# Backward of single-query attention: the V request moved between the two dV stores of a head, and the last V loaded in one piece

## The chip, the cores and the metric

One core of one Trainium2 chip, alone; the experiments ran on three chips (3, 7 and 10), each session beside the kernel before. The metric is the device time of one execution in microseconds (us). A core issues transfers through a queue (SP); the queue's transfers run on 16 DMA engines. A transfer of 128 partitions is 128 packets in the trace, eight for each engine, and sixteen semaphore increments, one from each engine.

## The reference, cut to what matters

```python
# q, grad_out: (1, 32, 1, 128); k, v: (1, 32, 8192, 128); all bf16
def fwd(q, k, v):
    scores = einsum('bhqd,bhkd->bhqk', q, k) * 128 ** -0.5
    attn = softmax(scores)
    return einsum('bhqk,bhkd->bhqd', attn, v)
out, vjp = jax.vjp(fwd, q, k, v)
return (out, *vjp(grad_out))        # out, dq, dk, dv
```

For each of 32 heads 2 MiB of K and 2 MiB of V are read and 2 MiB of dK and 2 MiB of dV are written: 268 MB in all.

## The kernel before

K and V tiles hold 64 rows in each of 128 partitions, so a partition's share of a load is one run of 16 KiB. Stores go in halves: 1 MiB, 8 KiB for each partition.

```python
K_BUFS, V_BUFS, NST = 3, 2, 2
def load_v(h):
    Vt[h] = vpool.tile([P, NT, D], BF16, tag="V", name="Vt")
    parts = NCH if h in (0, H - 1) else 1            # first and last V in four loads
    for c in range(parts):
        nc.sync.dma_start(slots(Vt[h], c, parts), rows_of(v, h, c, parts))

def outer(h, which, r):       # VectorE makes a quarter of dK or dV; after quarters 1 and 3 one half is stored
    ...
    if r % (4 // parts) == 4 // parts - 1:
        nc.sync.dma_start(rows_of(dst, h, c, parts), slots(G, c, parts))

for h in range(H + 1):        # ... marks cuts
    p_ = h - 1
    for u in range(NCH): k_blocks(h, u)              # VectorE transposes K
    k_scores(h)                                      # 64 small matmuls
    if 0 < h < H - 1: load_v(h + 1)
    ds_of(p_); outer(p_, "dk", 0); dq_of(p_, 0)      # 32 small matmuls
    s_mask(h); s_swap(h)
    dq_of(p_, 1); outer(p_, "dk", 1)                 # 32 small matmuls; first dK store
    if 0 < h and h + 2 < H: load_k(h + 2)
    ...                                              # softmax; dk 2, dk 3 and the second dK store
    v_transposes(h, 0)
    contract(Vt[h], x["p"], x["m"][:, 2:3])          # p times V: 64 small matmuls
    nc.scalar.copy(o_all[:, h:h + 1], x["m"][:, 2:3])
    v_transposes(h, 1)
    ...                                              # v_scores 0 to 3 (16 small matmuls each), transposes 2, 3
    outer(h, "dv", 0); outer(h, "dv", 1)             # first dV store
    outer(h, "dv", 2); outer(h, "dv", 3)             # second dV store
```

"Small" matmuls have 1, 2 or 4 columns and each comes with its own weight load of 128x128.

Of the kernel before, what the change touches and what calls it, by code (L numbers as in the profile page):

```python
# [24 lines left out]
def kernel(  # L25
# [13 lines left out]
    _, H, S, D = k.shape  # L39
    assert D == P and S % (P * CH) == 0 and H <= P  # L40
    NT = S // P
    NCH = NT // CH
# [20 lines left out]
    def rows_of(x, h, c, parts):  # L63
        L = NT // parts
        return x[0, h].rearrange("(p n) d -> p n d", p=P)[:, c * L:(c + 1) * L, :]

    def slots(X, c, parts):
        L = NT // parts
        return X[:, c * L:(c + 1) * L, :]

    def load_k(h):
        Kt[h] = kpool.tile([P, NT, D], BF16, tag="K", name="Kt")
        parts = NCH if h == 0 else 1
        for c in range(parts):
            nc.sync.dma_start(slots(Kt[h], c, parts), rows_of(k, h, c, parts))

    def load_v(h):
        Vt[h] = vpool.tile([P, NT, D], BF16, tag="V", name="Vt")
        parts = NCH if h in (0, H - 1) else 1
        for c in range(parts):  # L80
            nc.sync.dma_start(slots(Vt[h], c, parts), rows_of(v, h, c, parts))

# [54 lines left out]
    def k_blocks(h, u):  # L137


        if u == 0:  # L140
            XK[h] = ktpool.tile([P, CH, NB, NCH, QD], F32, tag="XK", name="XK_sb")
        nc.vector.transpose(XK[h][:, :, :, u, :],  # L142
                            slots(Kt[h], u, NCH).rearrange("p g d -> p (g d)").bitcast(F32).rearrange(
                                "p (g w j) -> p g w j", g=CH, w=NB))

    def k_scores(h):
        x = st[h]
        x["s"] = psS.tile([P, 512], F32, tag="s", name="s_ps")
        out = x["s"][:, 0:NT].rearrange("p (a g) -> p g a", a=NQ)
        cols = XK.pop(h).rearrange("p g w u i -> p (g w u i)").bitcast(BF16).rearrange(  # L150
            "p (g w ui e) -> p g w e ui", g=CH, w=NB, e=2)
        for g in range(CH):
            for c in range(2 * NB):
                nc.tensor.matmul(out[:, g, :], lhsT=cols[:, g, c // 2, c % 2], rhs=q_blk[:, h, c, :],  # L154
                                 start=(c == 0), stop=(c == 2 * NB - 1), skip_group_check=True)

    def s_mask(h):
        x = st[h]
        x["sm"] = small.tile([P, NQ, NCH, CH], F32, tag="sm", name="sm")
        nc.vector.tensor_tensor(  # L160
            x["sm"][:], x["s"][:, 0:NT].rearrange("p (a g) -> p a g", a=NQ).unsqueeze(2)
            .to_broadcast([P, NQ, NCH, CH]),
            in_quad[:].unsqueeze(1).unsqueeze(3).to_broadcast([P, NQ, NCH, CH]), op=ALU.mult)

    def s_swap(h):

        x = st[h]
        x["sn"] = x["s"][:, 128:128 + NT]
        for a in range(NQ):
            nc.tensor.matmul(x["s"][a * QD:(a + 1) * QD, 128:128 + NT], lhsT=lane[:],  # L170
                             rhs=x["sm"][:, a].rearrange("p u g -> p (u g)"),
                             start=True, stop=True, skip_group_check=True)
# [22 lines left out]
    def contract(Xt, rep, out_col, first=0, last=NT):  # L195
        for n in range(first, last):
            nc.tensor.matmul(out_col, lhsT=Xt[:, n, :], rhs=rep[:, n, 0:1],  # L197
                             start=(n == 0), stop=(n == NT - 1), skip_group_check=True)

    def outer(h, which, r):  # L200
        x = st[h]
        if r == 0:
            x[which] = gpool.tile([P, NT, D], BF16, tag=which, name="G_" + which)
        G, dst = x[which], out_2 if which == "dk" else out_3
        rep, row = x["ds"] if which == "dk" else x["p"], x["qd"][:, 0 if which == "dk" else 1, :]
        Q = NT // 4
        nc.vector.tensor_tensor(  # L207
            slots(G, r, 4).rearrange("p n (a b) -> p n a b", b=R),
            slots(rep, r, 4).unsqueeze(2).to_broadcast([P, Q, D // R, R]),
            row.rearrange("p (a b) -> p a b", b=R).unsqueeze(1).to_broadcast([P, Q, D // R, R]),  # L210
            op=ALU.mult)
        parts = 4 if h == H - 1 else NST
        if r % (4 // parts) == 4 // parts - 1:
            c = r // (4 // parts)
            nc.sync.dma_start(rows_of(dst, h, c, parts), slots(G, c, parts))
# [9 lines left out]
    def ds_of(h):  # L225
        x = st[h]
        pdt = small.tile([P, 1], F32, tag="pdt")
        nc.vector.tensor_copy(pdt[:], x["m"][:, 1:2])  # L228
        x["ds"] = small.tile([P, NT, R], BF16, tag="dsrep", name="ds_rep")
        nc.vector.scalar_tensor_tensor(  # L230
            out=x["ds"][:], in0=x["dp"][:, 0:NT].unsqueeze(2).to_broadcast([P, NT, R]), scalar=pdt[:],
            in1=x["p_s"][:].unsqueeze(2).to_broadcast([P, NT, R]), op0=ALU.subtract, op1=ALU.mult)

    def dq_of(h, half):
        out = st[h]["dp"][:, 128:129]
        contract(Kt[h], st[h]["ds"], out, half * NT // 2, (half + 1) * NT // 2)
        if half == 1:
            nc.scalar.copy(dq_all[:, h:h + 1], out)  # L238

    for h in range(H + 1):  # L240
        p_ = h - 1
        if h < H:
            x = st[h] = {}
            for u in range(NCH):
                k_blocks(h, u)
            k_scores(h)
            if 0 < h < H - 1:
                load_v(h + 1)
        if h > 0:
            ds_of(p_)  # L250
            outer(p_, "dk", 0)
            dq_of(p_, 0)
        if h < H:
            s_mask(h)
            s_swap(h)
        if h > 0:
            dq_of(p_, 1)
            outer(p_, "dk", 1)
        if 0 < h and h + 2 < H:
            load_k(h + 2)  # L260
        if h < H:
            mx = small.tile([P, 1], F32, tag="mx")
            nc.vector.reduce_max(mx[:], x["sn"], axis=AX.X)
            diag = small.tile([P, P], F32, tag="diag")
            nc.vector.tensor_scalar(diag[:], ident_f[:], mx[:], scale, op0=ALU.mult, op1=ALU.mult)
            x["m"] = psM.tile([P, 512], F32, tag="m", name="m_ps")
            nc.tensor.matmul(x["m"][:, 128:256], lhsT=ones_f[:], rhs=diag[:], start=True, stop=True,  # L267
                             skip_group_check=True)
            rows_bc(h)
        if h > 0:  # L270
            outer(p_, "dk", 2)
        if h == 0:
            load_k(2)
        if h < H:
            nbias = small.tile([P, 1], F32, tag="nbias")
            nc.vector.tensor_reduce(nbias[:], x["m"][:, 128:256], axis=AX.X, op=ALU.max, negate=True)  # L276
            e = small.tile([P, NT], F32, tag="e")
            rs = small.tile([P, 1], F32, tag="rs")
            nc.scalar.activation(e[:], x["sn"], ACT.Exp, bias=nbias[:], scale=scale, accum_out=rs[:])  # L279
            nc.tensor.matmul(x["m"][:, 0:1], lhsT=ones_f[:], rhs=rs[:], start=True, stop=True,  # L280
                             skip_group_check=True)
        if h > 0:
            outer(p_, "dk", 3)
        if h == H:
            break
        rinv = small.tile([P, 1], F32, tag="rinv")
        nc.vector.reciprocal(rinv[:], x["m"][:, 0:1])  # L287
        x["p"] = small.tile([P, NT, R], BF16, tag="prep", name="p_rep")
        nc.scalar.activation(x["p"][:], e[:].unsqueeze(2).to_broadcast([P, NT, R]), ACT.Copy, scale=rinv[:])  # L289
        x["p_s"] = small.tile([P, NT], F32, tag="p_s", name="p_s")  # L290
        nc.vector.tensor_scalar(x["p_s"][:], e[:], rinv[:], scale, op0=ALU.mult, op1=ALU.mult)
        v_transposes(h, 0)
        contract(Vt[h], x["p"], x["m"][:, 2:3])
        nc.scalar.copy(o_all[:, h:h + 1], x["m"][:, 2:3])
        v_transposes(h, 1)
        nc.tensor.matmul(x["m"][:, 1:2], lhsT=do_f[:, h:h + 1].to_broadcast([P, P]), rhs=o_all[:, h:h + 1],
                         start=True, stop=True, skip_group_check=True)
        v_scores(h, 0)
        v_transposes(h, 2)
        v_scores(h, 1)  # L300
        v_transposes(h, 3)
        v_scores(h, 2)
        v_scores(h, 3)
        outer(h, "dv", 0)
        outer(h, "dv", 1)
        outer(h, "dv", 2)
        outer(h, "dv", 3)

# [40 lines left out]
```

## Time and profile before

| | before |
|---|---|
| median of 4 runs | 663.08 us (662.32 to 663.71) |
| moved | 269.8 MB, 407 GB/s over the span |
| busiest compute engine | VectorE, 78% |
| a head in the steady part | 20.4 us |

The prediction below shows the DMA rows of the page, the stretches, the queue's waits and one head of the queue (start in us, duration in us, engine, line, operation, destination and sources, count), and says how to read them. One more view is needed for what follows. It is the trace's timeline of TensorE (start in us, duration in us, engine, line, operation, destination and sources, sizes, count), at the same head:

```profile
316.56 0.55 PE L192 MATMUL dp_ps<-do_blk,XT_sb 128*128 128x2 bf16 x16 [0.78 <-ACT XT_sb L182]
...
318.32 1.87 PE L154 MATMUL s_ps<-q_blk,XK_sb 128*128 128x4 bf16 x64 [1.21 <-DVE pdt L228]
320.05 0.99 PE L197 MATMUL dp_ps<-ds_rep,Kt 128*128 128x1 bf16 x32
320.97 0.44 PE L170 MATMUL s_ps<-sm,lane 128*32 128x64 f32 x8
321.34 1.01 PE L197 MATMUL dp_ps<-ds_rep,Kt 128*128 128x1 bf16 x32
```

From 318.3 to 322.3 us TensorE starts 136 matmuls and as many weight loads: some 68 instructions for each us. This is the densest stage of a head; I did not look at it when I predicted.

### The profile page before, as it was taken

The numbers are of one execution on the slowest core, as the hardware profiler recorded it, in microseconds if no ns is written. First come the engines' busy times: TensorE is split into PE (matmuls) and PEld (weight loads), VectorE is DVE, ScalarE is ACT, GpSimd is POOL, SyncE is SP. The second block draws the span as 40 slices with busy tenths as digits, with TensorE's granted clock in tenths as the row PEclk, the third lists the DMA queues.
The fourth block names the chain that finished last, engine by engine and source line by source line (L and its number), as shares of the span: only waits on it lengthen the run. The fifth ranks groups of instructions, "written<-read, shape, count | busy, mean of one in ns | idle before, by whom it ended". The sixth has DMA issues, their size and how long they took to land.

```text
span 662.2 us, 21100 instructions
## 1 busy us (share of the span) xinstructions
PE 505.4 (76%) x9705; PEld 470.8 (71%) x9705; DVE 513.4 (78%) x664; ACT 182.4 (28%) x321; POOL 0.7 (0%) x6
## 2 busy tenths in 40 slices
PE   2889888798887777878768687787877877768881
PEld 1878788688787766767668676677766777657871
DVE  5789788889987797777977778777788777786852
ACT  0332223223333222232222322223322323222330
POOL 0000000000000000000000000000000000000000
PEclk9955565757766576665567655666556665576655
DMA  8999999999999999999999999999999999999783
GB/s 335 410 424 427 426 421 422 423 423 427 427 425 426 426 424 427 427 428 424 426 422 428 426 426 429 420 428 415 413 423 418 414 416 415 396 424 402 290 355 144
DMA packets 29800, 269.83 MB, mean 407 GB/s; under 512 B 3472, under 2 KB 3472, under 8 KB 6032
## 3 DMA queue, kind: packets, MB, share of 16 engines
q1 hardware_dynamic: 29712, 268.48, 97.1%
q8 instruction: 76, 1.25, 0.7%
q14 instruction: 12, 0.10, 0.0%
HBM read 134.23 MB, written 134.23 MB: 405 GB/s over the span
## 4 chain that ended last, share of the span: by engine, by line
DMA 70%; PE 21%; DVE 3%; ACT 2%; issue 1%; SPq 0%; ACTq 0%
DMA Kt<-in_k_dram 26%; DMA Vt<-in_v_dram 25%; DMA out_dram<-G_dv 19%; PE T_ps L180 9%; PE s_ps L154 2%; PE m_ps L197 2%; PE dp_ps L197 2%; PE dp_ps L192 2%; ACT XT_sb L182 1%; DVE XK_sb L142 1%; PE m_ps L267 1%; PE m_ps L280 1%; DVE G_dk L207 1%; ACT e L279 1%; ACT qd L223 1%
## 5 line engine op out<-in xcount | busy, mean ns | idle before, releaser
L180 PE MATMUL T_ps<-ident_f,Vt 128*128 128x128 f32 x1024 | 222.6, 390 | 30.9 <-DMA Vt<-in_v_dram 30.8
L180 PEld LDWEIGHTS T_ps<-ident_f,Vt 128*128 128x128 f32 x1024 | 183.9, 208 | 32.1 <-issue 30.0
L142 DVE STREAM_TRANSPOSE XK_sb<-Kt 128x1024 f32<-128x1024 f32 x128 | 148.1, 1213 | 72.4 <-DMA Kt<-in_k_dram 72.3
L182 ACT COPY XT_sb<-T_ps 128x1024 f32<-128x1024 f32 x128 | 129.7, 1013 | 178.3 <-PE T_ps L180 178.3
L207 DVE TENSOR_TENSOR G_dk<-ds_rep,qd 128x2048 bf16<-128x2048 bf16 x128 | 155.7, 1219 | 1.1
L207 DVE TENSOR_TENSOR G_dv<-p_rep,qd 128x2048 bf16<-128x2048 bf16 x128 | 148.2, 1220 | 9.0 <-ACT p_rep L289 9.0
L192 PEld LDWEIGHTS <-XT_sb 128*128 128x128 bf16 x2048 | 73.3, 103 | 29.5 <-ACT XT_sb L182 27.5
L192 PE MATMUL dp_ps<-do_blk,XT_sb 128*128 128x2 bf16 x2048 | 71.6, 164 | 24.7 <-ACT XT_sb L182 24.7
L154 PE MATMUL s_ps<-q_blk,XK_sb 128*128 128x4 bf16 x2048 | 58.4, 167 | 28.8 <-DVE pdt L228 26.1
L154 PEld LDWEIGHTS <-XK_sb 128*128 128x128 bf16 x2048 | 55.8, 101 | 30.7 <-DVE pdt L228 27.9
L197 PE MATMUL dp_ps<-ds_rep,Kt 128*128 128x1 bf16 x2048 | 64.4, 165 | 7.1 <-issue 6.4
L197 PEld LDWEIGHTS <-Kt 128*128 128x128 bf16 x2048 | 59.7, 103 | 12.6 <-issue 12.4
L197 PEld LDWEIGHTS <-Vt 128*128 128x128 bf16 x2048 | 62.5, 105 | 2.0
L197 PE MATMUL m_ps<-p_rep,Vt 128*128 128x1 bf16 x2048 | 60.5, 166 | 0.0
L238 ACT COPY dq_all<-dp_ps 128x1 f32<-128x1 f32 x32 | 5.1, 159 | 178.2 <-PE dp_ps L197 178.2
L280 PEld LDWEIGHTS m_ps<-rs,ones_f 128*128 128x128 f32 x64 | 16.0, 311 | 48.6 <-ACT e L279 48.6
L280 PE MATMUL m_ps<-rs,ones_f 128*128 128x1 f32 x64 | 18.7, 362 | 39.2 <-ACT e L279 39.2
L276 DVE TENSOR_REDUCE nbias<-m_ps 128x1 f32<-128x128 f32 x32 | 9.3, 292 | 24.3 <-ACT qd L223 24.3
L267 PE MATMUL m_ps<-diag,ones_f 128*128 128x128 f32 x64 | 25.5, 499 | 2.2 <-issue 1.3
L230 DVE SCALAR_TENSOR_TENSOR ds_rep<-dp_ps,pdt,p_s 128x256 bf16<-128x256 f32 x32 | 15.5, 484 | 14.0 <-PE dp_ps L192 11.8
L289 ACT ACTIVATE p_rep<-e,rinv 128x256 bf16<-128x256 f32 x32 | 16.2, 508 | 30.3 <-DVE rinv L287 30.3
L223 ACT CAST qd<-m_ps 128x256 bf16<-128x256 f32 x32 | 11.9, 373 | 44.8 <-PE m_ps L219 44.8
(44 smaller groups left out, 161.0 us busy)
## 6 DMA issues: line engine op xcount, KB each, us to landing
Kt<-in_k_dram SPq DMA_DIRECT2D x31, 2048.0 KB, 27.7
out_dram<-G_dv SPq DMA_DIRECT2D x62, 1024.0 KB, 25.6
out_dram<-G_dk SPq DMA_DIRECT2D x62, 1024.0 KB, 27.8
Vt<-in_v_dram SPq DMA_DIRECT2D x30, 2048.0 KB, 28.1
Vt<-in_v_dram SPq DMA_DIRECT2D x8, 512.0 KB, 13.7
Kt<-in_k_dram SPq DMA_DIRECT2D x4, 512.0 KB, 5.1
out_dram<-G_dv SPq DMA_DIRECT2D x4, 512.0 KB, 16.8
out_dram<-G_dk SPq DMA_DIRECT2D x4, 512.0 KB, 10.3
```

Source lines behind the costliest of these rows:

```text
L142: nc.vector.transpose(XK[h][:, :, :, u, :], slots(Kt[h], u, NCH).rearrange("p g d -> p (g d)").bitcast(F32).rearrange("p (g w j) -> p g w ...
L154: nc.tensor.matmul(out[:, g, :], lhsT=cols[:, g, c // 2, c % 2], rhs=q_blk[:, h, c, :], start=(c == 0), stop=(c == 2 * NB - 1), skip_group ...
L180: nc.tensor.transpose(T_ps[:, i, :], words[:, m * P:(m + 1) * P], ident_f[:])
L182: nc.scalar.copy(X[:], T_ps[:])
L192: nc.tensor.matmul(st[h]["dp"][:, n:n + 2], lhsT=X[:, i, e2, :], rhs=do_blk[:, h, e2, :], start=(e2 == 0), stop=(e2 == 1), skip_group_chec ...
L197: nc.tensor.matmul(out_col, lhsT=Xt[:, n, :], rhs=rep[:, n, 0:1], start=(n == 0), stop=(n == NT - 1), skip_group_check=True)
L207: nc.vector.tensor_tensor(slots(G, r, 4).rearrange("p n (a b) -> p n a b", b=R), slots(rep, r, 4).unsqueeze(2).to_broadcast([P, Q, D // R, ...
L223: nc.scalar.copy(x["qd"][:].rearrange("p a d -> p (a d)"), x["m"][:, 256:512])
L230: nc.vector.scalar_tensor_tensor(out=x["ds"][:], in0=x["dp"][:, 0:NT].unsqueeze(2).to_broadcast([P, NT, R]), scalar=pdt[:], in1=x["p_s"][: ...
L267: nc.tensor.matmul(x["m"][:, 128:256], lhsT=ones_f[:], rhs=diag[:], start=True, stop=True, skip_group_check=True)
L280: nc.tensor.matmul(x["m"][:, 0:1], lhsT=ones_f[:], rhs=rs[:], start=True, stop=True, skip_group_check=True)
L289: nc.scalar.activation(x["p"][:], e[:].unsqueeze(2).to_broadcast([P, NT, R]), ACT.Copy, scale=rinv[:])
```

## The change

Its intent: V(h+2) is asked for as soon as V(h)'s buffer can be free, ahead of the second dV store, and the queue alternates loads and stores better. The last V no longer needs to come in pieces.

```diff
     def load_v(h):
-        parts = NCH if h in (0, H - 1) else 1
+        parts = NCH if h == 0 else 1
@@
             k_scores(h)
-            if 0 < h < H - 1:
-                load_v(h + 1)
@@
         outer(h, "dv", 0)
         outer(h, "dv", 1)
+        if h + 2 < H:
+            load_v(h + 2)
         outer(h, "dv", 2)
         outer(h, "dv", 3)
```

## The prediction

> **What bounds the kernel now.** I read the page's DMA rows first: 268 MB pass through one core, and no compute engine is above 78% busy.
>
> ```profile
> span 662.2 us, 21100 instructions
> DMA  8999999999999999999999999999999999999783
> GB/s 335 410 424 427 426 421 422 423 423 427 427 425 426 426 424 427 427 428 424 426 422 428 426 426 429 420 428 415 413 423 418 414 416 415 396 424 402 290 355 144
> q1 hardware_dynamic: 29712, 268.48, 97.1%
> q8 instruction: 76, 1.25, 0.7%
> ```
>
> The plateau is some 425 GB/s with every DMA engine over 90% busy; the last slices fall off. At 425 GB/s 268.5 MB take 632 us, so 30 us seem to be lost, and the fall at the end looks like where. The second view, stretches of the trace with the DMA share and GB/s last, shows what that fall is:
>
> ```profile
> 165.00:440.00 275.00, 212.14 (x4104) 197.98 (x4103) 216.83 (x272) 79.06 (x139) 0.00 (x0) 0.61 1.01 426
> 440.00:590.00 150.00, 113.83 (x2265) 106.06 (x2261) 117.22 (x150) 39.77 (x71) 0.00 (x0) 0.59 1.01 415
> 655.00:660.00 5.00, 0.00 (x0) 0.00 (x0) 0.00 (x0) 0.00 (x0) 0.00 (x0) 0.50 0.06 26
> ```
>
> At 655 to 660 us one engine of 16 (share 0.06 = 1/16) still moves 26 GB/s, its full rate, and the other fifteen are done. So I grouped the trace's semaphore increments from DMAs in sixteens, one for each DMA engine of a transfer. The last increment of each transfer trails the fifteenth by 0.15 us at 14.7 us, 3.0 us at 204 us, 7.5 us at 389 us, 11.1 us at 594 us and 6.7 us at the end; the earliest is 20 us ahead by 460 us. One DMA engine is late for the whole run, and no transfer counts as landed before it. The landings of that engine follow each other without a hole from 14.7 us to 660.9 us: about 2.5 us for a 1 MiB store, 4.9 us for a 2 MiB load, up to 6.3 us where instruction fetches fall in.
>
> Its work can be added up. Each engine carries 1/16: 64 loads x 8 packets of 16 KiB and 128 stores (counted as 1 MiB) x 8 packets of 8 KiB. The trace's packets last 611 and 309 ns at the median and overlap by 4 ns: 512 x 0.607 + 1024 x 0.305 = 623 us, and some 2 us for 209 semaphore packets. The 76 fetch packets never overlap one another; beside one of them a store packet typically lasts 0.70 us and a load packet 1.10 us, so about 0.45 us is lost at each, 34 us in all if one engine takes them (not shown by a record, but the sum fits): 623 + 2 + 34 = 659, after a start at 1.7 us gives 660.9. The last bulk landing is at 660.9. This engine has no idle time to win.
>
> The third view is the DMA queue's own waits, 165 to 590 us (total us, times, longest):
>
> ```profile
> SPq L215 <- DMA Kt<-in_k_dram: 93.6, 21, 5.1
> SPq L215 <- DMA out_dram<-G_dk: 91.1, 42, 2.3
> SPq L75 <- DMA Vt<-in_v_dram: 86.8, 20, 4.5
> SPq L215 <- DMA out_dram<-G_dv: 52.9, 21, 2.6
> SPq L81 <- DMA out_dram<-G_dv: 46.2, 21, 2.9
> SPq L215 <- DVE mx L263: 3.2, 5, 2.0
> ```
>
> Nearly all of it is one transfer waiting for another, not for compute. The program has eight DMA semaphores in turn, so transfer n waits for transfer n-8 to land. One head of the steady state as the queue issues it:
>
> ```profile
> 313.68 2.99 SPq L215 DMA_DIRECT2D out_dram<-G_dv  x2
> 318.88 0.34 SPq L81 DMA_DIRECT2D Vt<-in_v_dram  x1
> 321.81 0.33 SPq L215 DMA_DIRECT2D out_dram<-G_dk  x1
> 326.67 0.34 SPq L75 DMA_DIRECT2D Kt<-in_k_dram  x1
> 329.20 0.33 SPq L215 DMA_DIRECT2D out_dram<-G_dk  x1
> ```
>
> A head lasts 20.42 us (313.68 to the next at about 334.1, and the same spacing for most heads), while a clean one costs a DMA engine 16 x 0.607 + 32 x 0.305 = 19.5 us; the 0.9 us between them is 76/32 = 2.4 fetches. At each issue seven older transfers are still pending, 23 to 25 us of work for the late engine.
>
> **What the Trainium skill says.** "DMA: Bandwidth & Descriptors", section "Why a DMA increments its semaphore by 16 and not by 1": every participating engine posts its own increment and only the full 16 means landed. The trace agrees, and the spread of those sixteen is the 11 us above. Same page, "Issuing engines are not separate DMA queues": all issued DMAs end on the same 16 engines; so order in the queue cannot make bandwidth. "Perfetto Trace Analysis", section "Roofline", puts one core alone at the 16 engines' aggregate of about 435 GB/s; the plateau here is 426. "Runtime: NRT & Kernel Launch", section "Instruction fetch mechanics": each sequencer refills its instructions in 16 KiB blocks of 256 through a DMA queue of its own. The trace agrees with the block (76 packets, 1.25 MB); the page calls the cost mostly hidden, which is true for the sequencer but not, by the sum above, for the late DMA engine.
>
> **The change, part by part.** I compared the built instruction streams. PE, DVE and ACT keep every instruction in its place; only the semaphores that they wait on are renumbered. So fetch traffic is the same, 0 us.
>
> 1. "Two heads ahead" is a new name for almost the same place. Before, V of head h+1 was issued in head h after K's scores, and the queue ran dV(h-1), dV(h-1), V(h+1), dK(h-1). Now it runs dV, V, dV, dK: one 2 MiB load passes one 1 MiB store. Bytes and packets are the same. In steady state V lands about 2.5 us earlier and the second dV half 4.9 us later. The late engine sees the same sum in another order: 0 us.
>
> 2. The wait for V's buffer. V(h+2) takes the buffer of V(h), free after PE's last transposes of head h. Early in the run this holds the queue: the first dV store is issued at 22.72 us, V at 28.58. The second dV half, which went at about 25, must now wait for 28.9. Does an engine run dry? At 28.6 us the fastest engine has just finished the third K (landings 28.8 to 31.4) and has dV's first half, 2.5 us, to go; V is then in the queue. In the next head V is issued at 47.7 while about 3 us (fastest) to 6 us (late engine) remain. Later the backlog grows. No hole: 0 us, at worst under 1 us once, on engines that have slack later.
>
> 3. G_dv's buffers. DVE may write G_dv(h) only when both stores of head h-2 have landed. The second one landed about 4.3 us before it was needed in steady state (321.7 against 326.06); now it lands about 4.9 us later, so DVE may wait about 0.5 us for it. DVE sat idle for 3.4 us before K's transposes and dV's issue comes 8 us later, so this is hidden.
>
> 4. The last V in one load instead of four. Three fewer transfers: three semaphore packets of some 10 ns each. It also frees the queue at the end, which before spent 10.65 us on it:
>
> ```profile
> 594.07 0.34 SPq L75 DMA_DIRECT2D Kt<-in_k_dram  x1
> ...
> 606.70 10.65 SPq L81 DMA_DIRECT2D Vt<-in_v_dram  x4
> 621.93 2.93 SPq L215 DMA_DIRECT2D out_dram<-G_dk  x2
> ...
> 646.92 4.44 SPq L215 DMA_DIRECT2D out_dram<-G_dk  x4
> ```
>
> The dK stores at 621.93 waited for the last K to land; eight places on there is now another transfer, so they should go at about 610. That feeds the fifteen fast engines earlier, not the late one, which has its backlog anyway. The final chain is K landed (621.89), transposes, scores, V's transposes at 633.39, dK, last store at about 651. Is the unsplit V there in time? On the late engine after K at 621.87 follow dK's half (2.6), dV's half (2.6), V (4.9): about 632.0, 1.4 us before PE wants it. And were it late, the last store goes out at 651 while the late engine has work until 660.9: some 9 us of slack.
>
> Sum: 0 + 0 + 0 + 0, with a few tenths either way. I take 663.3 us against 663.4.
>
> **The rivals.**
> (a) The end is bound by compute and the unsplit V delays it. For: the page's chain ends in K's landing, PE and DVE work, and the split was there for that. Against: 9 us of slack on the late engine. It would take a V over 10 us late; say 665 to 668.
> (b) The holes in the last slices are starvation by the queue, and freeing it wins. For: 290 and 144 GB/s, and 12 us of earlier dK stores. Against: one engine at 26 GB/s to the very end. If the fetches moved with the order of transfers or the late engine did have holes, up to 10 us could come: 653.
> (c) V's buffer wait in front of the second dV half starves the DMA in the first 165 us, where the queue waits for compute. For: the wait exists (up to 4 us at a time). Against: the backlog of 3 us and more. A loss of 1 us in each of 8 heads would give 671.
>
> **Range and chances.** Three runs before lie between 662.32 and 663.71; with half a microsecond for steps 2 and 3 and for another session I take 661.7 to 665.0. Over 2% would mean beyond 650 or 677, further than any rival is likely to reach: faster 0.01, same 0.97, slower 0.02.
>
> **What would show it.** Right: 20.4 us for a steady head; one engine at 26 GB/s at the end; the median landing time of dK stores down by up to 2.5 us and of dV stores up by as much; dK stores near 610 us instead of 621.93; the DMA row full from the second slice. Wrong: a slice below 400 GB/s before 150 us (c), PE waiting for the last V after 634 us and the last store after 660 (a), or the late engine done before 655 (b).

## The result, and the profile after

| | before | changed |
|---|---|---|
| median | 663.08 us | 657.43 us (656.14 to 658.36) |
| ratio | | 0.9914, 95% interval 0.9893 to 0.9935 |

Ratios are computed as the mean time of one kernel's runs over that of the other's of the same rounds, so they are not quite the ratio of the medians. By the 2% rule the two are the same, as forecast; but the gain of 5.7 us is clear of the noise and lies outside my range of 661.7 to 665.0.

First the changed kernel's page, the rows that answer to those of before:

```profile
span 656.6 us, 21096 instructions
GB/s 334 408 389 428 424 422 430 420 423 430 424 424 428 425 428 423 428 424 427 428 424 426 428 424 425 428 428 423 428 425 424 431 421 426 419 418 412 374 339 149
q8 instruction: 76, 1.25, 0.7%
```

The third slice fell from 424 to 389 GB/s (a hole at the start), bytes and fetches are the same, and the plateau now stays near 424 until the 36th slice, where before it had sagged to 415 from the 28th on. Then the same stretches (DMA share and GB/s last):

```profile
165.00:440.00 275.00, 222.40 (x4135) 208.07 (x4136) 219.93 (x276) 79.00 (x140) 0.00 (x0) 0.56 1.01 426
440.00:590.00 150.00, 121.25 (x2266) 112.98 (x2264) 118.67 (x151) 41.30 (x76) 0.00 (x0) 0.53 1.01 424
651.00:654.00 3.00, 0.00 (x0) 0.00 (x0) 0.00 (x0) 0.00 (x0) 0.00 (x0) 0.50 0.06 26
```

Still one DMA engine of sixteen works alone at the end, at its full 26 GB/s. So the bound is the one that I had named. It simply finished 5.7 us earlier. The queue's timeline of one head says where (the lines of before have 20.4 us from head to head):

```profile
313.14 0.33 SPq L215 DMA_DIRECT2D out_dram<-G_dv  x1
315.75 0.34 SPq L81 DMA_DIRECT2D Vt<-in_v_dram  x1
318.27 0.33 SPq L215 DMA_DIRECT2D out_dram<-G_dv  x1
323.12 0.33 SPq L215 DMA_DIRECT2D out_dram<-G_dk  x1
325.65 0.34 SPq L75 DMA_DIRECT2D Kt<-in_k_dram  x1
328.42 0.33 SPq L215 DMA_DIRECT2D out_dram<-G_dk  x1
333.27 0.33 SPq L215 DMA_DIRECT2D out_dram<-G_dv  x1
```

A head now takes 333.27 - 313.14 = 20.13 us. The landings of K add it up: from K of head 9 to K of head 31 the kernel before needs 621.9 - 170.8 = 451.1 us and the changed one 616.9 - 172.0 = 444.9, 6.2 us less over 22 heads. K of head 9 itself is 1.2 us later, and the rest after head 31 is 0.7 us shorter.

To see which transfer got cheaper I took, for each transfer, the last of its sixteen semaphore increments, and the step from one transfer's last increment to the next: the time that the late engine spent on it. Near 310 to 330 us:

```
before:  V 4.86   dK 2.53   K 4.91   dK 2.65   dV 2.54   dV 2.91     sum 20.40
changed: dK 2.60  dV 2.52   V 4.85   dV 2.53   dK 2.75   K  4.86     sum 20.11
clean:   a load 8 x 0.607 = 4.86, a store 8 x 0.305 = 2.44           sum 19.48
```

Loads cost their clean time to within 0.05 us. Nearly everything above it, 0.9 us before and 0.6 us now, is lost in stores, and in the kernel before half of it in one store, the second dV half. That half was being moved from about 318.3 to 321.2 us (an increment comes some 0.5 us after its last packet), which is TensorE's densest stage shown above. In the changed kernel TensorE's timeline reads:

```profile
317.78 1.87 PE L154 MATMUL s_ps<-q_blk,XK_sb 128*128 128x4 bf16 x64 [1.52 <-DVE pdt L228]
319.51 0.99 PE L197 MATMUL dp_ps<-ds_rep,Kt 128*128 128x1 bf16 x32
320.43 0.44 PE L170 MATMUL s_ps<-sm,lane 128*32 128x64 f32 x8
320.80 1.01 PE L197 MATMUL dp_ps<-ds_rep,Kt 128*128 128x1 bf16 x32
...
326.28 1.89 PE L197 MATMUL m_ps<-p_rep,Vt 128*128 128x1 bf16 x64
```

The dense stage, 317.8 to 321.8 us, now lies under the V load (the late engine moved it from 317.7 to 322.6), and the second dense stage, p times V at 326.3 to 328.2, under the first dK store (325.1 to 327.8), whose step is now the dearest, 2.75 us.

Packets of one DMA engine follow each other without a gap, so the eight packets of a transfer on the late engine can be followed back from its last increment (some that could not be followed are left out). Sorted by the number of TensorE matmuls and weight loads that start while a packet lasts, their mean duration in ns (number of packets):

```
instructions started     0-7         8-21        22-29       30 or more
store 8 KiB, before      318 (469)   339 (147)   357 (177)   388 (47)
store 8 KiB, changed     317 (601)   337 (83)    350 (129)   389 (11)
load 16 KiB, before      613 (217)   620 (37)    611 (32)    620 (106)
load 16 KiB, changed     614 (131)   619 (47)    620 (60)    614 (162)
```

On this engine a store packet gets up to 22% longer in TensorE's dense stages (388 against 318 ns), a load packet 1% at most. The changed order moved dense stages from stores to loads: store packets with 22 or more went from 224 to 140. An instruction fetch somewhere on the 16 engines does not slow it: before, its store packets beside a fetch lasted 333 ns (70 of them), without one 334 ns; and none of its steps from 130 to 550 us is longer by as much as a fetch packet (0.9 us): the longest store step there is 3.28 us.

### The profile page after: what moved, and what is told of

It reads as the page before. It is cut to its first block, busy times and chain, and to the rows that moved or that the text cites. A ratio compares the mean times of both kernels' runs of the same rounds, so it can differ in the third digit from the quotient of the medians. Undisturbed runs are those within 1.5% of the kernel's fastest.

```text
span 656.6 us, 21096 instructions
## 1 busy us (share of the span) xinstructions
PE 520.1 (79%) x9705; PEld 485.8 (74%) x9705; DVE 513.8 (78%) x664; ACT 182.2 (28%) x321; POOL 0.7 (0%) x6
## 4 chain that ended last, share of the span: by engine, by line
DMA 63%; PE 23%; DVE 8%; ACT 2%; issue 1%; SPq 0%; ACTq 0%; DVEq 0%
DMA Kt<-in_k_dram 35%; DMA out_dram<-G_dv 29%; PE T_ps L180 10%; DVE XK_sb L142 6%; PE s_ps L154 3%; PE dp_ps L197 2%; PE m_ps L197 2%; PE dp_ps L192 2%; ACT XT_sb L182 1%; PE m_ps L265 1%; PE m_ps L278 1%; DVE G_dk L207 1%; ACT e L277 1%; ACT qd L223 1%; PE s_ps L170 1%
## 5 line engine op out<-in xcount | busy, mean ns | idle before, releaser
L180 PE MATMUL T_ps<-ident_f,Vt 128*128 128x128 f32 x1024 | 237.8, 410 | 0.0
L180 PEld LDWEIGHTS T_ps<-ident_f,Vt 128*128 128x128 f32 x1024 | 198.8, 222 | 0.0
L207 DVE TENSOR_TENSOR G_dv<-p_rep,qd 128x2048 bf16<-128x2048 bf16 x128 | 148.2, 1220 | 14.0 <-DMA out_dram<-G_dv 10.7
L192 PEld LDWEIGHTS <-XT_sb 128*128 128x128 bf16 x2048 | 77.5, 107 | 30.2 <-ACT XT_sb L182 27.1
L192 PE MATMUL dp_ps<-do_blk,XT_sb 128*128 128x2 bf16 x2048 | 73.8, 166 | 24.3 <-ACT XT_sb L182 24.3
L265 PE MATMUL m_ps<-diag,ones_f 128*128 128x128 f32 x64 | 25.6, 500 | 2.3 <-issue 1.7
## 6 DMA issues: line engine op xcount, KB each, us to landing
out_dram<-G_dv SPq DMA_DIRECT2D x62, 1024.0 KB, 25.3
out_dram<-G_dk SPq DMA_DIRECT2D x62, 1024.0 KB, 25.3
```

The lines of the kernel that those rows point to most:

```text
L180: nc.tensor.transpose(T_ps[:, i, :], words[:, m * P:(m + 1) * P], ident_f[:])
L192: nc.tensor.matmul(st[h]["dp"][:, n:n + 2], lhsT=X[:, i, e2, :], rhs=do_blk[:, h, e2, :], start=(e2 == 0), stop=(e2 == 1), skip_group_chec ...
L207: nc.vector.tensor_tensor(slots(G, r, 4).rearrange("p n (a b) -> p n a b", b=R), slots(rep, r, 4).unsqueeze(2).to_broadcast([P, Q, D // R, ...
L265: nc.tensor.matmul(x["m"][:, 128:256], lhsT=ones_f[:], rhs=diag[:], start=True, stop=True, skip_group_check=True)
```

## The experiments

The theory: one DMA engine, always the same, sets the end; its stores, and not its loads, slow down while TensorE starts many instructions. (The increments carry no engine number. That the last one is always the same engine's is read from its lag, which grows smoothly from about 125 us on in both kernels.) Rivals: the unsplit last V made the gain; the instruction fetches of the prediction slow the late engine; the exchange of order matters in itself; a busy TensorE slows it, whatever its instructions. Twelve kernels ran.

**The change in two halves.** First the new order with the last V still in four loads.

```diff
-        parts = NCH if h == 0 else 1
+        parts = NCH if h in (0, H - 1) else 1
```

> The new order alone, the last V still in four loads. Theory: on the DMA engine that lands last, a store packet takes 309 ns while TensorE starts few instructions and up to 389 ns in its dense stages, a load packet 611 ns always; the new order puts a V load under the densest stage, so the steady head falls from 20.4 to 20.1 us and the whole gain comes from here: 657 to 658 us. Rival: the gain comes from the unsplit last V, which frees the queue at the end: then 663 us here.

Measured: 657.15 us, ratio to before 0.9909 (0.9894 to 0.9923). Then the other half, in the kernel before:

```diff
-        parts = NCH if h in (0, H - 1) else 1
+        parts = NCH if h == 0 else 1
```

> The old order, the last V in one load. Theory: 663 us, the steady head stays at 20.4 us. Rival (the unsplit last V makes the gain): 657 to 658 us.

Measured: 663.24 us, ratio 1.0002 (0.9988 to 1.0017). The whole gain comes from the order; the last V is worth nothing.

**TensorE moved, the queue left alone.** In the changed kernel one group of transposes goes ahead of p times V:

```diff
         v_transposes(h, 0)
+        v_transposes(h, 1)
         contract(Vt[h], x["p"], x["m"][:, 2:3])
         nc.scalar.copy(o_all[:, h:h + 1], x["m"][:, 2:3])
-        v_transposes(h, 1)
```

> The changed kernel with one exchange on TensorE alone: the second group of V transposes goes before the 64 small matmuls of p times V. The DMA queue keeps its order, and instructions, bytes and fetches are the same. Theory: those matmuls move by 1.8 us, from under the first dK store (step 2.75 us on the late engine) to under the K load, so that step falls to about 2.5 us, the head from 20.13 to 19.9 us, the whole by 4 to 6 us against the changed kernel: 652 to 654 us. Rivals (instruction fetches slow the late engine; or only the order of transfers counts): no change, 657 to 658 us.

Measured: 653.75 us, ratio 0.9867 (0.9846 to 0.9888), 3.7 us under the changed kernel (ratios 0.9867 against 0.9914). Its TensorE timeline at another head:

```profile
303.19 3.59 PE L180 MATMUL T_ps<-ident_f,Vt 128*128 128x128 f32 x16
306.61 1.76 PE L197 MATMUL m_ps<-p_rep,Vt 128*128 128x1 bf16 x64
```

The 64 small matmuls start at 306.6; the K load is moved from about 306.4 to 311.3 us (the first dK half has its last increment at 306.86, K at 311.78). The first dK store's mean step between 250 and 590 us fell from 2.79 to 2.53 us and the other stores stayed within 0.03. Not one instruction, byte or fetch was added or taken away.

The same exchange in the kernel before is the control:

> Control: the same exchange on TensorE (second group of V transposes before the 64 matmuls of p times V) in the kernel before. There these matmuls already lie under the K load, about 1.5 us after its start, and stay under it when they move by 1.8 us. Theory: no change, 663 us within 1.5. Rival (the exchange is good for TensorE or ScalarE in itself, whatever the DMA moves): 659 to 660 us, as with the changed kernel.

Measured: 662.66 us, ratio 0.9989 (0.9973 to 1.0006): no change, as expected, since there p times V lay under the K load already. So the exchange is not good in itself.

**Which engine is late.** In the changed kernel one store was cut into 16:

```diff
+            if h == 24 and which == "dv" and c == 0:
+                p0 = 0
+                for n in (15, 14, 13, 12, 11, 10, 9, 8, 7, 6, 5, 4, 3, 2, 1, 8):
+                    nc.sync.dma_start(rows_of(dst, h, c, parts)[p0:p0 + n], slots(G, c, parts)[p0:p0 + n])
+                    p0 += n
```

> One 1 MiB store of head 24 cut by partitions into 16 stores of 15, 14, 13 ... 1 and 8 partitions, to learn by their landings on which of the 16 DMA engines the late one is: a store of n partitions takes n engines[...]. Those with the late engine should land about 8 us after the others' level, those without it early. Time within 2 us of the changed kernel, 656 to 659 us. If no single engine is late (rival: the lateness moves from engine to engine), the landings show no such edge.

Measured: 661.51 us (one run), slower than expected, because the small stores used up the eight places of the queue and the backlog ran out. The stores of 15 down to 9 partitions all had one late increment, so the late engine is one of the numbers 0 to 8; below that nothing could be read. The second probe keeps the backlog:

```diff
+            if 17 <= h <= 24 and which == "dv" and c == 0:
+                for n in (h - 16, 32 - h, 112):     # n, 16-n and 112 partitions
+                    nc.sync.dma_start(...[p0:p0 + n], ...[p0:p0 + n])
```

> A second probe for the number of the late DMA engine (the first leaves 0 to 8, because its small stores let the backlog run out), on the changed kernel with the exchange: in heads 17 to 24 the first dV store is cut into n, 16-n and 112 partitions, n = 1 to 8, so that the backlog stays. The smallest store that has an increment 4 us or more after all others tells the number. Time 654 to 658 us.

Measured: 663.28 us (one run), again slower than I expected. The landings answer the question. The stores of 1, 2, 3 and 4 partitions were complete 12.4, 10.5, 8.5 and 7.7 us before the whole dK store that was issued ahead of them, so the late engine had no part in them; that of 5 partitions had its last increment 6.9 us after the one before it, and landed level with the late engine (458.90 us, between dK at 458.60 and the next piece at 459.23). With the rule that the Trainium skill gives ("DMA: Bandwidth & Descriptors", section "Why a DMA increments its semaphore by 16 and not by 1": the lowest-numbered k engines), the late engine is number 4. The trace agrees with the rule as far as it shows it: one increment for each partition of these small stores, and one more at once.

**More of the disputed work, under loads or under stores.** Twins with p times V run twice for each head, in one under the K load, in the other under stores:

```python
# the order after the edit; ... marks cuts
# under the load                          # under the stores
v_transposes(h, 0)                        contract(... [:, 2:3])
v_transposes(h, 1)                        contract(... [:, 3:4])   # not used
contract(... [:, 2:3])                    nc.scalar.copy(o_all ...)
contract(... [:, 3:4])   # not used       v_transposes(h, 0)
nc.scalar.copy(o_all ...)                 v_transposes(h, 1)
```

> Changed kernel; the 64 small matmuls of p times V are run twice (the second result is not used), both after the second group of V transposes, so from 3.6 to 7.1 us after the softmax, under the K load. 2048 more matmuls with their weight loads, some 16 more instruction fetches. Theory: a load packet does not mind TensorE, so about the time of the exchange alone plus a little for the longer chain of compute: 653 to 657 us. Rival (fetches, or the number of TensorE instructions in itself, slow the late engine): the same as its twin with both under the stores.

Measured: 695.92 us, ratio 1.0502 (1.0456 to 1.0549).

> Twin of the other: the same instructions, both runs of the 64 matmuls before the first V transposes, from the softmax's end to 3.5 us later, under the second dV store and the first dK store. Theory: the late engine loses about 0.25 us more for each steady head than in the changed kernel (its dK step 2.8 us and its dV step 2.7 us or more), 661 to 666 us, 5 to 10 us over the twin. Rival: no difference between the twins.

Measured: 667.53 us, ratio 1.0063 (1.0048 to 1.0078). The opposite of the forecast, and no test of the theory, because the bound changed. The chain that ended last in the twin under the load, shares by engine:

```profile
PE 81%; ACT 9%; DVE 5%; issue 3%; DMA 1%; SPq 0%; DVEq 0%; ACTq 0%
```

In both the queue waited for compute (in the first for V's transposes 249.9 us in 30 waits, in the second 225.4 us in 30), and near 310 us the late engine was only 0.2 to 0.7 us behind the fifteenth in the first, 2.7 to 3.4 us in the second. I had counted on 1.5 us of idle TensorE for 1.7 us of added work. The pair says only that there is no room for more compute.

**Less of it.** With 1 of the 64 matmuls left (wrong results), first in the kernel before:

```diff
-        contract(Vt[h], x["p"], x["m"][:, 2:3])
+        nc.tensor.matmul(x["m"][:, 2:3], lhsT=Vt[h][:, 0, :], rhs=x["p"][:, 0, 0:1], start=True, stop=True, ...)
```

> Wrong result on purpose: in the kernel before, only 1 of the 64 matmuls of p times V is left for each head (2016 matmuls and as many weight loads fewer, some 15 instruction fetches fewer). In its steady state these matmuls lie under the K load. Theory: the late engine gains little, 661 to 663.5 us. Rival (fetches, or the number of TensorE instructions, slow the late engine): 15 fetches of 0.45 us, 656 to 657 us.

Measured: 658.04 us, ratio 0.9925 (0.9911 to 0.994). More than I expected, and near the rival's number.

> The same cut in the changed kernel, where these matmuls lie under the first dK store. Theory: that store's step on the late engine falls from 2.8 to about 2.5 us, the whole by 4 to 6 us against the changed kernel, 651 to 654 us, a larger gain than in the kernel before. Rival: the same gain in both kernels.

Measured: 646.39 us, ratio 0.9746 (0.973 to 0.9763): 11 us under the changed kernel, 5.9 us more than the same cut saved in the kernel before. The rival asks for the same gain in both and falls by that. The mean steps of the late engine show what happened (us, transfers landing between 250 and 590):

```
                     dK 1st  dK 2nd  dV 1st  dV 2nd   V     K
before               2.57    2.68    2.59    2.92     4.86  4.92
before, one matmul   2.53    2.60    2.50    2.93     4.86  4.90
changed              2.79    2.61    2.57    2.50     4.87  4.88
changed, exchange    2.53    2.61    2.60    2.51     4.87  4.90
changed, one matmul  2.45    2.47    2.54    2.53     4.95  4.93
```

In both, the shorter TensorE chain also pulled the bursts of V scores forward, out of the second dK and first dV half (0.08 and 0.09 us in the kernel before, whose whole head fell from 20.54 to 20.32 us, 4.8 us over 22 heads). That term I had left out. The second dV half under the densest stage stayed at 2.93 us although 16 fetches and 4032 TensorE instructions were gone. In the last row the late engine is hardly late any more: near 320 us it is 0.2 us behind the fifteenth, against 3.3 us in the changed kernel, and its store packets last 310 ns at the mean.

**The cost by itself.** A kernel without the attention: the queue always full of 1 MiB stores from one tile, with compute in stages.

```diff
+    for _ in range(16): store()
+    g = gate(1)                       # a small load that starts the next stage when it lands
+    for _ in range(16): store()
+    for _ in range(1200): nc.tensor.matmul(ps[:, 0:1], lhsT=g[:], rhs=wide[:, 0:1], ...)
+    ...                               # 90 matmuls of 512 columns; 300 VectorE, 150 ScalarE copies of one column
+    for n in range(9): nc.sync.dma_start(X[:], rows_of(k, n, 0, 1))       # loads, with 1200 small matmuls
```

> The disputed cost by itself (outputs wrong on purpose): stages of 16 stores of 1 MiB, the DMA queue always full. Stage 1: all compute idle. Stage 2: TensorE runs 128x1 matmuls, each with its weight load. Stage 3: TensorE runs 128x512 matmuls, busy but with few instructions. Stage 4: VectorE runs tiny copies. Stage 5: ScalarE runs tiny copies. Stage 6: 2 MiB loads beside TensorE's 128x1 matmuls. Stage 7: stores, idle. Theory: the late engine's store packets last 309 ns in stages 1, 3 and 7 and 370 to 390 ns in stage 2, load packets 611 ns in stage 6; the other fifteen engines stay at 309 ns in stage 2. Stages 4 and 5 are open: if instructions of these engines count too, another DMA engine or the same one falls behind there. Rival (a busy TensorE, not its instructions): stage 3 as slow as stage 2. Rival (fetches): slow only in the few packets beside a fetch.

Measured: 297.99 us (one run, outputs wrong). Its stretches: idle, small matmuls, wide matmuls, VectorE, loads beside small matmuls:

```profile
5.00:40.00 35.00, 0.00 (x0) 0.00 (x0) 0.00 (x0) 0.00 (x0) 0.00 (x0) 1.00 1.01 418
46.00:106.00 60.00, 31.89 (x1160) 31.41 (x1158) 0.00 (x0) 0.00 (x0) 0.00 (x0) 1.00 1.01 415
108.00:126.00 18.00, 18.00 (x80) 7.91 (x79) 0.00 (x0) 0.00 (x0) 0.00 (x0) 1.00 1.01 420
130.00:166.00 36.00, 0.00 (x0) 0.00 (x0) 29.40 (x192) 0.00 (x0) 0.00 (x0) 0.51 1.01 422
216.00:254.00 38.00, 21.43 (x772) 21.01 (x770) 0.00 (x0) 0.00 (x0) 0.00 (x0) 0.50 1.01 423
```

The sum over 16 engines hides it; the lateness of the last engine behind the first does not:

```
stage                          window of landings    late at its start and end
stores, compute idle           7.0 to 44.6 us        0.2 -> 0.3 us
stores, small matmuls          56.6 to 106.7         2.2 -> 4.8
stores, wide matmuls           109.2 to 126.7        4.7 -> 4.8
stores, VectorE copies         129.2 to 174.5        4.7 -> 4.9
stores, ScalarE copies         180.1 to 202.6        5.5 -> 5.5
loads, small matmuls           215.0 to 254.3        4.2 -> 4.2
stores, small matmuls ending   257.1 to 265.2        4.4 -> 5.3
stores, compute idle           267.7 to 294.7        5.3 -> 5.3
```

The small matmuls come in bursts of 128 (27 ns apart) with stalls of 3.6 us between them; in a burst the late engine's store packets last 370 to 389 ns, in the stall, where the fetch falls, 309 ns. TensorE busy all the time with wide matmuls does nothing, nor do VectorE or ScalarE, nor small matmuls beside loads. Two things do not fit so neatly. In the first 10 us of the small-matmul stage the lateness jumped by 2 us in two transfers (steps 2.98 and 3.89 us), and two engines were far behind for a while. And one single store lost 0.6 us at 177.6 us, beside VectorE's and ScalarE's copies; that stays open.

The trace explains the first. The step of 3.89 us holds the first fetch (at 51.41 us, 0.96 us long), and the engine that fell to 2.3 us behind the first then came slowly nearer, while another, 0.9 us behind at 50.3 us and 1.3 at 56.6, fell steadily back to 4.8. So the 2.2 us at the start of the second row are those of an engine that took a fetch; the late one went from 1.3 to 4.8. Fetches do have a price: all 19 here (0.88 to 1.11 us long) are followed by one slow packet, a store of 674 to 718 ns or a load of 1079 to 1159 ns. By 250 us, after sixteen fetches, seven engines were within 0.42 us of the first, eight were 1.6 to 2.7 us behind it, and the late one 4.2. The reading that fits is that other engines take the fetches in turn and the late one takes none.

**The best version.** The exchange of TensorE, and in head 0 alone the V request after both dV stores again:

```diff
-        if h + 2 < H:
+        if 0 < h and h + 2 < H:
             load_v(h + 2)
         outer(h, "dv", 2)
         outer(h, "dv", 3)
+        if h == 0:
+            load_v(h + 2)
```

> The changed kernel with the exchange on TensorE, and in head 0 alone the V request after both dV stores, as in the kernel before. Theory: the changed kernel lost 1.3 to 1.7 us once at about 30 us, where the late engine waited for V (step 6.55 us against 4.9); this takes it back: 652 to 653 us, against 653.75 with the exchange alone. Rival (the backlog later hides that hole): no difference.

Measured: 653.25 us, ratio 0.9852 (0.9837 to 0.9866). The long step of this V is gone in the trace (4.87 us at about 41 us, against 6.08 in the profiled run of the exchange alone and 6.55 in the changed kernel), but the next V, at 59.5 us, now has one of 6.15 us, against 4.91 with the exchange alone. So the wait was in good part moved by one head: K of head 9 landed at 170.2 us, against 170.9. The two intervals overlap, and by the times it is not told apart from the exchange alone. Both beat the changed kernel and the kernel before.

## Why the prediction was wrong

- **The bound was right.** One late DMA engine, to the last store; compute and the queue only follow. Of the views that I named for it, one engine at 26 GB/s at the end, the dK stores near 610 us, dK's landing time and the full DMA row came out so. The head of 20.4 us (20.1) and dV's landing time did not.
- **The step that failed is the first of the change's parts**: "The late engine sees the same sum in another order: 0 us." A store's cost on that engine depends on what TensorE does at that moment, so the order changes the sum. (The page that the prediction cites says only that all transfers end on the same 16 engines; that their order then cannot matter was my own step.) The second dV half fell from 2.92 to 2.50 us at the mean and the first dK half rose from 2.57 to 2.79; with smaller terms the steady head lost 0.28 us, 6.2 us over 22 heads.
- **Behind it stands a wrong term in the sum**: I gave the late engine the median packet of all sixteen, 309 ns for a store, and filled the 34 us that were missing with 76 fetches of 0.45 us. The sum met 660.9 us almost exactly, by chance; and 2.4 fetches of 0.45 us for each head would be 1.1 us, not the 0.9 that they were to explain. In truth its own store packets last 334 ns at the mean (of those followed). In the steady part none of its steps has room for a fetch. The engine that takes one pays the fetch packet of 0.9 us as well as the 0.45. The text said that no record showed the fetches on this engine; the packets could have been sorted by engine before, from the same trace. Nor was one engine late for the whole run: before about 125 us others were last for a while, and the step of 6.3 us that I took for the late engine's (K at 89.9 us) set an engine 1.5 us further back at a fetch (86.1 us). The 11 us that the prediction calls the spread of the sixteen increments is the lag of the last behind the fifteenth; the whole spread at 594 us is 21 us.
- **The V buffer wait** (second part) was forecast as no hole or under 1 us. It made one: the step to V's last landing at 40.4 us is 6.55 us, and the K landing of head 9 is 1.2 us later. The term was mis-sized. The 389 GB/s slice shows it, and that is the sign that I had named for rival (c).
- **G_dv's buffers** (third part): VectorE waited for a dV landing 10.7 us in all, 20 times, 0.5 us each as forecast, without effect.
- **The unsplit last V** (fourth part): 0 us, as forecast. The dK stores went at 606.8 us instead of 621.9, near the 610 that I gave, and it bought nothing. dK's median landing time fell from 27.8 to 25.3 us as forecast; dV's did not rise (25.6 to 25.3).
- **The rivals**: none of the three was it. Rival (c) happened once, for some 1.2 us, and not in eight heads. Rival (b) had named "holes" of the late engine; it had none, it was slowed.

What stays open is why. No run shows what TensorE's instructions and the stores of DMA engine 4 share. Every small matmul here has its own weight load, so many instructions and many weight loads are not told apart: the stage of wide matmuls has few of both. A late engine appears in the traces of all three chips, but its number was read on one of them (chip 10), and every trace is of core 0. Nor can these runs tell whether the recording of the profile has a part in it.

## What to carry to other kernels

When transfers bind, look at the sixteen DMA engines one by one: the spread of a transfer's semaphore increments shows whether one is late, and the sum of its own packets, not of the median packet, is the bound. If a late engine's stores are slowed by dense small matmuls, put loads under those matmuls, by the order of the queue or by the order on TensorE; the second cost one exchanged line here and gave another 3.7 us. And a sum that meets the measured time exactly is no proof of its terms.

## What the Trainium skill lacked or had wrong

- "DMA: Bandwidth & Descriptors", section "Latency and other measured facts", names engines 7 and 15 as usually slower, and its best guess at the cause concerns only transfers issued by GpSimd. For transfers issued by SP, as here, it names no slower engine. Here it was number 4 in the probe, and in the kernel before the late engine was up to 12.6 us behind the fifteenth.
- No page has it that stores on one DMA engine slow down beside dense TensorE instructions; "SBUF — State Buffer", section "SBUF: two separate sides", even says that a compute op cannot slow a DMA. Measured here: 8 KiB store packets 317 ns with few instructions and 389 ns with 30 or more; 16 KiB load packets 611 to 620 ns always. Whether the two meet in SBUF or elsewhere no run shows.
- "Runtime: NRT & Kernel Launch", section "Instruction fetch mechanics", calls crossing a 16 KiB block mostly hidden. With the DMA queue full and one small matmul after another, TensorE stalled some 3.6 us after every 128 matmuls (256 instructions), so it was not hidden there. Nor does it say what a fetch costs the DMA engine that takes it: 0.88 to 1.11 us, and a slow packet after it.
